# The row maximum of the attention scores in two reductions instead of one, with the score tile kept fixed

## The chip, the cores and the metric

The kernel runs on one core of one Trainium2 chip. The metric is the device time of one execution in microseconds; less is better. Before the change the median of three runs is 1004.71 us (1004.12 to 1005.11). The core has five engines that run side by side and wait for one another through semaphores: TensorE (PE, with weight loads shown as PEld), VectorE (DVE), ScalarE (ACT), GpSimd (POOL) and SyncE (SP), which issues most of the transfers (DMA).

## The reference

One block of a network over 2048 tokens of width 640: a layer norm with a modulation from a conditioning vector, attention in a sliding window of 256 tokens with 32 heads of 20 columns, a projection, a second layer norm, and a two-layer MLP with 1536 hidden columns. The part that matters here:

```
qkv = (x @ wqkv).reshape(B, S, 3, H, Dh)          # H = 32 heads, Dh = 20
scores = einsum("bhqd,bhkd->bhqk", q, k) * (Dh ** -0.5)
mask = (idx[:, None] - idx[None, :] >= 0) & (idx[:, None] - idx[None, :] < W)   # W = 256
p = softmax(where(mask, scores, -1e9))
o = einsum("bhqk,bhkd->bhqd", p, v)
...
x = x + ga * (o @ wo)
x = x + gb * MLP(layernorm(x) * (1 + cb) + sb)
```

The softmax needs the maximum of every row of the masked scores.

## The kernel before, in words

The work falls into a prologue (the first columns of q and k), an attention phase, and the MLP. In the attention phase the tokens come in two halves of 1024, the heads in eight quads of four, and the queries in blocks of 128. One step `t` of the main loop takes one block of queries of one quad. There are 128 such steps, and three things overlap in a step:

- `s_batch` (tile `s`): the scores of 128 queries against up to 384 keys, for four heads, by TensorE into PSUM. `s_max` then masks them on VectorE (`copy_predicated`, the mask of the block that leaves the window) and reduces them to the row maximum `nm` with one `tensor_reduce` over 256 columns of each of four heads (the 128 columns of the first key block are folded in by the masking copy).
- `e_batch` (tile `e`): 11 steps later (`LAG`), the same scores transposed, keys on the partitions, with the negated maximum brought in through two further rows of q. `e_mask` masks on VectorE, `e_exp` takes the exponential on ScalarE into `pt`, and GpSimd masks two further blocks.
- `pv_stage` (tile `o`): the product of `pt` with the values.

The rest of TensorE's time in a step goes to the projections of later columns (`pp`, `ppo`), which a plan spreads over the steps by tables of numbers (`EXTRA`, `EARLY`, `AFTER` and others). Neither the plan nor the tables are touched. Everything is recorded in program order on each engine, so an instruction that waits holds up all that stands behind it on its engine.

From step 11 to step 127 (117 steps) `width()` gives 384, and the tiles `s` and `e` have 4 x 384 = 1536 columns of 4 bytes each, which is three PSUM banks of 512 columns. Head slots 0 to 3 start at columns 0, 384, 768 and 1152. So slot 1 lies in banks 0 and 1, slot 2 in banks 1 and 2, and slot 3 wholly in bank 2. `cuts` splits a product where it crosses a bank. There is one tile `s` and one tile `e`: the products of the next step write the same columns that the reduction of this step reads.

The slots 0 and 1 use rows 0 to 59 (61 for `e`) of TensorE's array, the slots 2 and 3 rows 64 and up, so two products at a time can run side by side. `score_batch` orders them by the list `BOTH`. In a step with both tiles that gives, on TensorE's queue: three products of `e`, two of `s` (first 256 columns in bank 1, then 384 columns in bank 2), three of `e`, four of `s`. Where a step has no `e`, the list `ONE` gives six of `s`, and the first two are the same. Tiles are asked from a pool for every step, and the first product into a new tile waits for what used the old one (`reuse_waits="tile"`).

Of the kernel before, what the change touches and what calls it, by code (L numbers as in the profile page):

```python
# [9 lines left out]
F32 = mybir.dt.float32  # L10
# [3 lines left out]
ALU = mybir.AluOpType  # L14
AX = mybir.AxisListType
PSUM = bass.MemoryType.PSUM

P = 128
# [47 lines left out]

SUMS_LAST = [14, 18, 25, 31, 32, 42, 43, 46, 50, 52, 55, 58, 60, 61, 62, 63, 76, 77, 78, 79, 88, 90, 91, 94, 95, 99, 101, 102, 103, 105, 108, 109, 110, 111, 115, 116, 117, 120, 122, 126, 127, 131, 132, 133, 136, 139]
LEAST = 4
MOST = 10
MODS = [[9.5, 17.0], [16.75, 27.5], [70.5, 79.0]]  # L70
WOS = [88.75, 91.75, 99.25, 110.25, 112.0, 113.25, 116.0]
# [53 lines left out]
def block_kernel(ctx: ExitStack, tc: tile.TileContext, x, wqkv, wo, w1, b1, w2, b2, c, crow, wmod, wcol, sel, outT):  # L125
    core = tc.nc
    nc = Ordered(tc)
# [75 lines left out]
    pools = {}  # L203
# [327 lines left out]

    def score_banks(kind, name):
        n = width()
        t = pools[kind].tile([P, 4 * n], F32, tag=kind, name=name)
        return t, t.rearrange("p (h n) -> p h n", n=n)[:, :, 0:384]

    def width():
        return 384 if LAG <= now[0] < 2 * NQB * QUADS else 512  # L540
# [10 lines left out]
    def score_batch(batches):  # L551

        cut = []
        for n, (t, parts) in enumerate(batches):
            cut.append([
                [(n, at // 512, t[:, at:to], lhs, rhs(off, to - at)) for col, size, lhs, rhs in part for at, to, off in cuts(slot, col, size)]  # L560
                for slot, part in enumerate(parts)
            ])
        both = [{m[1] for m in c[0] + c[1]} & {m[1] for m in c[2] + c[3]} for c in cut]
        own = lambda n, slot: [m for m in cut[n][slot] if m[1] not in both[n]]
        shared = lambda n, slot: [m for m in cut[n][slot] if m[1] in both[n]]

        kinds = {
            (n, k): go
            for n in range(len(batches))
            for k, go in zip("abcdef", (shared(n, 0) + shared(n, 1), own(n, 1), own(n, 0), own(n, 3), own(n, 2), shared(n, 2) + shared(n, 3)))  # L570
        }
        order = BOTH if len(batches) == 2 else ONE
        queue = [(int(k in "def"), mm) for n, k in order for mm in kinds.get((int(n), k), ())]
        given = {}
        for i, (half, mm) in enumerate(queue):
            n, bank, out, lhs, rhs = mm
            if half and (n, bank) in given:
                assert not [1 for h, m in queue[i:] if not h and m[:2] == (n, bank)]
                tc.add_manual_dep(
                    nc.tensor.nop().ins, given.pop((n, bank)).name, in_order, reason="rows of the array share a bank"  # L580
                )
            ins = matmul(out, lhs, rhs, start=True, stop=True).ins
            if not half and bank in both[n]:
                given[n, bank] = ins

# [18 lines left out]
    def s_max(it, s, c0):  # L604

        data = negc.to_broadcast([P, 4, P]) if c0 else s[:, :, 0:P]
        nc.vector.copy_predicated(s[:, :, 2 * P : 384], masks["s"].to_broadcast([P, 4, P]), data)
        nc.vector.tensor_reduce(it["quad"]["nm"][:, :, it["key"][2]], s[:, :, max(c0, P) : 384], AX.X, ALU.max)

    def m_rows(it):  # L610
        half, quad, _, _ = it["key"]
# [561 lines left out]
    lo, hi = 4.0, 16.0  # L1173
    for _ in range(30):
        room = (lo + hi) / 2
        lo, hi = (lo, room) if lay_units(room)[0] <= LAST else (room, hi)
# [35 lines left out]
    for half in range(2):  # L1212
# [4 lines left out]
        for quad in range(QUADS):  # L1217
            if half or quad:
                js = range(4 * quad * DH // P, (4 * quad * DH + 4 * DH - 1) // P + 1)
                due = 8 * (half * QUADS + quad)  # L1220
                for c2 in range(2):
                    t = due + 4 * c2 - READ
                    for kind in range(2):
                        t = max([t, due - 8 * NSLOT + LAG + 8] + [over_at.get((kind, j, c2), -9) + 2 for j in js])
# [3 lines left out]
    for n, ((g, at), lo) in enumerate(zip(((2, 0), (4, 1), (3, 2)), MODS)):  # L1228
        steps, rows = mod_steps(g, at)
        spread(plan, [step(1, f) for f in steps], lo[0], lo[1])  # L1230
        t = int(lo[1])
        for f in rows:
            t = take_aside(t, f) + 1
    for ch, when in turns.items():
# [7 lines left out]
        t = when  # L1242
# [244 lines left out]
```

## Time and profile before

| | |
|---|---|
| median of 3 runs | 1004.71 us |
| the profiled execution's own time | 1004.25 us |
| its span, first to last instruction | 1002.5 us |
| busy: PE, PEld | 951.8 us (95%), 755.3 us (75%) |
| busy: DVE, ACT, POOL | 592.8 us (59%), 444.6 us (44%), 481.7 us (48%) |
| stretch 97 to 557 us (the 117 steps with three-bank tiles): PE, DVE busy | 433.80 us, 347.26 us of 460.00 |

How to read it: a line of the groups has the operation, its tiles as out<-in, shapes and count, then busy time, the mean of one in ns, and the idle time of the engine just before, with what ended it. A line of the timeline has start, length, engine and operation, and in brackets the idle time before it. Instructions next to each other with the same tiles are merged, with their count. All operations are recorded by one helper, so they all show as line L119 and are told apart by tiles. The busy time of PE contains ends that are modelled: a product that follows another closely overlaps it in the rows, so a short wait need not show as idle time.

### The profile page before, as it was taken

The numbers are of one execution on the slowest core, as the hardware profiler recorded it, in microseconds if no ns is written. First come the engines' busy times: TensorE is split into PE (matmuls) and PEld (weight loads), VectorE is DVE, ScalarE is ACT, GpSimd is POOL, SyncE is SP. The second block draws the span as 40 slices with busy tenths as digits, with TensorE's granted clock in tenths as the row PEclk, the third lists the DMA queues.
The fourth block names the chain that finished last, engine by engine and source line by source line (L and its number), as shares of the span: only waits on it lengthen the run. The fifth ranks groups of instructions, "written<-read, shape, count | busy, mean of one in ns | idle before, by whom it ended". The sixth has DMA issues, their size and how long they took to land.

```text
span 1002.5 us, 19950 instructions
## 1 busy us (share of the span) xinstructions
PE 951.8 (95%) x7737; PEld 755.3 (75%) x7737; DVE 592.8 (59%) x939; ACT 444.6 (44%) x781; POOL 481.7 (48%) x680
## 2 busy tenths in 40 slices
PE   8899999999999999999698879999999999999997
PEld 7777777777777677777476658888888888888886
DVE  6564867879677787767678644765444444433112
ACT  3724545566654544554345663343433343333122
POOL 4423655676864354644537844454543445442221
PEclk9999999999999999999899989999999999999999
DMA  8265878557678269834662144444422334124113
GB/s 301 91 215 144 280 239 263 169 163 212 198 231 260 86 178 277 234 101 159 190 184 67 52 127 136 154 131 139 132 86 84 94 129 127 40 64 147 53 45 113
DMA packets 99262, 152.81 MB, mean 152 GB/s; under 512 B 8897, under 2 KB 42145, under 8 KB 99169
## 3 DMA queue, kind: packets, MB, share of 16 engines
q1 hardware_dynamic: 89952, 143.16, 46.3%
q10 hardware_dynamic: 9216, 8.39, 2.6%
q8 instruction: 61, 1.00, 0.4%
q14 instruction: 33, 0.26, 0.1%
HBM read 99.17 MB, written 51.58 MB: 150 GB/s over the span
## 4 chain that ended last, share of the span: by engine, by line
PE 80%; DVE 9%; ACT 4%; issue 2%; DMA 2%; POOL 1%; SPq 0%; DVEq 0%; ACTq 0%; POOLq 0%
PE pp L119 16%; PE out L119 16%; PE h L119 16%; PE o L119 7%; PE e L119 7%; PE wo L119 6%; PE s L119 6%; DVE e L119 3%; ACT pt L119 3%; DVE nm L119 2%; PE ppo L119 2%; DVE s L119 1%; PE yt L119 1%; PE pv L119 1%; PE xt L119 1%
## 5 line engine op out<-in xcount | busy, mean ns | idle before, releaser
L119 POOL TENSOR_SCALAR_AFFINE_SELECT pt<-pt 128x512 f32<-128x512 f32 x192 | 129.2, 673 | 149.3 <-ACT pt L119 142.6
L119 ACT ACTIVATE pt<-e 128x1024 f32<-128x1024 f32 (+1 forms) x120 | 133.6, 1114 | 66.6 <-DVE e L119 63.3
L119 POOL TENSOR_TENSOR w2lo<-w2r,w2hi 128x640 fp32r<-128x640 f32 x48 | 75.8, 1580 | 166.9 <-ACT w2hi L119 166.7
L119 DVE TENSOR_REDUCE nm<-s 128x4 f32<-128x1024 f32 (+1 forms) x128 | 152.7, 1193 | 4.4
L119 PEld LDWEIGHTS e<-qbuf,kbuf 62*128 62x128 f32 x773 | 81.5, 188 | 57.5 <-ACT pt L119 33.1
L119 PE MATMUL e<-qbuf,kbuf 62*128 62x128 f32 (+2 forms) x773 | 108.0, 320 | 17.3 <-ACT pt L119 17.0
L119 PE MATMUL s<-kbuf,qbuf 60*128 60x128 f32 (+2 forms) x728 | 108.3, 312 | 10.3 <-DVE nm L119 7.4
L119 PE MATMUL pp<-hhi,whi 128*128 128x512 f32 x265 | 114.0, 430 | 0.9 <-ACT whi L119 0.7
L119 DVE COPY_PREDICATED e<-mask_t,e 128x512 f32<-128x512 uint32 x96 | 66.6, 694 | 77.5 <-PE e L119 66.8
L119 DVE CAST ghi<-g 128x512 fp32r<-128x512 f32 x48 | 27.1, 565 | 143.9 <-ACT g L119 143.8
L119 PE MATMUL pp<-hlo,whi 128*128 128x512 f32 x265 | 107.6, 406 | 3.1 <-POOL hlo L119 3.1
L119 PE MATMUL pp<-hhi,wlo 128*128 128x512 f32 x265 | 108.2, 408 | 0.0
L119 PE MATMUL o<-pt,vbuf 128*32 128x128 f32 x2688 | 102.1, 282 | 0.5 <-ACT oT L119 0.4
L119 PEld LDWEIGHTS s<-kbuf,qbuf 60*128 60x128 f32 x728 | 82.9, 187 | 21.7 <-DVE nm L119 5.4
L119 POOL TENSOR_TENSOR wlo<-wraw,whi 128x128 fp32r<-128x128 f32 x180 | 77.9, 463 | 39.9 <-ACT whi L119 32.0
L119 PE MATMUL out<-ghi,w2hi 128*128 128x512 f32 x240 | 96.2, 401 | 0.0
L119 PE MATMUL h<-yhi,w1hi 128*128 128x512 f32 x240 | 95.8, 399 | 0.0
L119 PE MATMUL out<-ghi,w2lo 128*128 128x512 f32 x240 | 94.1, 392 | 0.0
L119 PE MATMUL out<-glo,w2hi 128*128 128x512 f32 x240 | 94.0, 392 | 0.0
L119 PE MATMUL h<-ylo,w1hi 128*128 128x512 f32 x240 | 93.9, 391 | 0.0
L119 PE MATMUL h<-yhi,w1lo 128*128 128x512 f32 x240 | 93.9, 391 | 0.0
L119 ACT COPY oT<-o 128x128 f32<-128x128 f32 x128 | 33.8, 264 | 128.2 <-PE o L119 121.8
(169 smaller groups left out, 1840.8 us busy)
## 6 DMA issues: line engine op xcount, KB each, us to landing
w2r<-in_w SPq DMA_DIRECT2D x48, 320.0 KB
qbuf<-q_scr SPq DMA_DIRECT2D x60, 240.0 KB
wraw<-in_wqkv SPq DMA_DIRECT2D x37, 320.0 KB
kbuf<-k_scr SPq DMA_DIRECT2D x44, 240.0 KB
q_scr<-stage SPq DMA_DIRECT2D x20, 512.0 KB
k_scr<-stage SPq DMA_DIRECT2D x20, 512.0 KB
o_scr<-oT ACTq DMA_DIRECT2D x64, 128.0 KB
wm<-in_wmod SPq DMA_DIRECT2D x20, 320.0 KB
```

The costliest lines, as they stand in the source:

```text
L119: return self.tc.keep_in_program_order(op(*args, **kw))
```

## The change

Three things change, all for the steps in which `s` has three banks.

1. `s_max` reduces in two instructions: slots 0 to 2 (`CUT = 3`) and then slot 3. The columns read and the values written are the same.
2. The tile `s` is asked from its pool once and kept (`fixed`), so a step's products follow what they overlap in the tile and no longer a change of tile.
3. In `score_batch`, a product of `s` is declared free of a reduction that reads no bank which it writes. The first reduction reads columns 0 to 1151, banks 0 to 2. The second reads columns 1152 to 1535, bank 2. So the products into banks 0 and 1 stand behind the first reduction alone.

```diff
+CUT = 3
...
+    fixed, maxima = {}, []
+
     def score_banks(kind, name):
         n = width()
-        t = pools[kind].tile([P, 4 * n], F32, tag=kind, name=name)
+        if kind == "s" and n == 384:
+            if "s" not in fixed:
+                fixed["s"] = pools[kind].tile([P, 4 * n], F32, tag=kind, name=name)
+            t = fixed["s"]
+        else:
+            t = pools[kind].tile([P, 4 * n], F32, tag=kind, name=name)
         return t, t.rearrange("p (h n) -> p h n", n=n)[:, :, 0:384]
...
             ins = matmul(out, lhs, rhs, start=True, stop=True).ins
+            if n == len(batches) - 1 and width() == 384:
+                for red, banks in maxima:
+                    if bank not in banks:
+                        tc.declare_no_dep(ins, red, reason="no bank of the maximum")
...
-        nc.vector.tensor_reduce(it["quad"]["nm"][:, :, it["key"][2]], s[:, :, max(c0, P) : 384], AX.X, ALU.max)
+        del maxima[:]
+        n = width()
+        for lo, hi in ((0, CUT), (CUT, 4)) if n == 384 else ((0, 4),):
+            red = nc.vector.tensor_reduce(
+                it["quad"]["nm"][:, lo:hi, it["key"][2]], s[:, lo:hi, max(c0, P) : 384], AX.X, ALU.max
+            )
+            if n == 384:
+                maxima.append((red.ins, range(lo * n // 512, (hi * n - 1) // 512 + 1)))
```

What stands on VectorE's queue around one step of the second half (the reduction of step 109, the masks of step 110, `e1_4_3` and the scores behind it), before. The name in front of the arrow is what is written, and the bracket names the engines or transfers whose semaphores the instruction waits for:

```order
L119 COPY_PREDICATED e1_4_3_6328<-mask_t_73,e1_4_3_6328 128x4x128 [waits PE_49,Activation_49]
L119 COPY_PREDICATED s1_5_6_6329<-mask_t_73,s1_5_6_6329 128x4x128 [waits DVE_49,PE_49]
L119 TENSOR_REDUCE nm1_5_6034<-s1_5_6_6329 128x4 [waits DVE_49]
L119 COPY_PREDICATED e1_4_4_6400<-mask_t_73,e1_4_4_6400 128x4x128 [waits PE_49,Activation_49]
L119 COPY_PREDICATED s1_5_7_6401<-mask_t_73,s1_5_7_6401 128x4x128 [waits DVE_49,PE_49]
```

The same place after (the kept tile has the name of the step in which it was asked for, `s0_1_3`):

```order
L120 TENSOR_REDUCE nm1_5_6035<-s0_1_3_996 128x1
L120 COPY_PREDICATED e1_4_3_6329<-mask_t_73,e1_4_3_6329 128x4x128 [waits PE_49,Activation_49]
L120 COPY_PREDICATED s0_1_3_996<-mask_t_73,s0_1_3_996 128x4x128 [waits DVE_49,PE_49]
L120 TENSOR_REDUCE nm1_5_6035<-s0_1_3_996 128x3 [waits DVE_49]
L120 TENSOR_REDUCE nm1_5_6035<-s0_1_3_996 128x1
L120 COPY_PREDICATED e1_4_4_6401<-mask_t_73,e1_4_4_6401 128x4x128 [waits PE_49,Activation_49]
```

The second reduction waits for nothing of its own and stands directly behind the first; over the program VectorE has 117 instructions more.

TensorE's queue in the same step, before (`e1_4_3` is the transposed tile of this step, `s1_5_6` its scores, `qbuf` and `kbuf` hold q and k; `o1_4_0` is the product with the values that comes next):

```order
L119 MATMUL e1_4_3_6328<-qbuf0_96,kbuf0_99 128x128
L119 MATMUL s1_5_6_6329<-kbuf1_100,qbuf1_97 128x256 [waits DVE_49,PE_49]
L119 MATMUL s1_5_6_6329<-kbuf1_100,qbuf1_97 128x384
L119 MATMUL e1_4_3_6328<-qbuf0_96,kbuf0_99 128x128
L119 MATMUL e1_4_3_6328<-qbuf0_96,kbuf0_99 128x384
L119 MATMUL e1_4_3_6328<-qbuf0_96,kbuf0_99 128x256 [waits PE_49]
```

And after:

```order
L120 MATMUL e1_4_3_6329<-qbuf0_96,kbuf0_99 128x128
L120 MATMUL s0_1_3_996<-kbuf1_100,qbuf1_97 128x256 [waits DVE_49]
L120 MATMUL s0_1_3_996<-kbuf1_100,qbuf1_97 128x384 [waits DVE_49]
L120 MATMUL e1_4_3_6329<-qbuf0_96,kbuf0_99 128x128
L120 MATMUL e1_4_3_6329<-qbuf0_96,kbuf0_99 128x384
L120 MATMUL e1_4_3_6329<-qbuf0_96,kbuf0_99 128x256 [waits PE_49]
```

No product changes its place. The first score product loses its second wait (on TensorE's own semaphore) and keeps one on VectorE. The second score product, into bank 2, has a wait on VectorE of its own.

## The prediction

> **What bounds the kernel now.** I read the page first, then the stretch of the attention steps, then who waits for the reductions, then the timeline of single steps.
>
> ```profile
> span 1002.5 us, 19950 instructions
> PE pp L119 16%; PE out L119 16%; PE h L119 16%; PE o L119 7%; PE e L119 7%; PE wo L119 6%; PE s L119 6%; DVE e L119 3%; ACT pt L119 3%; DVE nm L119 2%; PE ppo L119 2%; DVE s L119 1%; PE yt L119 1%; PE pv L119 1%; PE xt L119 1%
> ```
>
> ```profile
> 97.00:557.00 460.00, 433.80 (x4861) 325.07 (x4862) 347.26 (x448) 243.35 (x453) 258.99 (x412) 0.99 0.64 193
> ```
>
> The second line is the chain of work that ended last. It is TensorE nearly throughout. Reductions (`DVE nm`) hold 2% of it, some 20 us or 16 of them at 1.23 us each. The third line is the stretch 97 to 557 us, in which the change acts (span, then busy PE, PEld, DVE, ACT, POOL): TensorE is idle for 26 us, VectorE for 113 us. So VectorE's load is not the bound. What counts is when a reduction lets TensorE go on.
>
> ```profile
>   PE s L119: 7.4, 14
>   PEld s L119: 5.4, 7
> ```
>
> These are the waits for `nm`: 12.8 us in 21 places. That understates it, since the ends of TensorE's products are modelled and cover short waits. I therefore paired each reduction's end with the first score product behind it. A step that is not held looks like this (VectorE's reduction, then on TensorE the first product of `e`, the first of `s`, the last of `e`):
>
> ```profile
> 299.69 1.23 DVE L119 TENSOR_REDUCE nm<-s 128x4 f32<-128x1024 f32 x1
> ...
> 301.02 0.45 PE L119 MATMUL e<-qbuf,kbuf 62*128 62x256 f32 x3
> 301.30 0.34 PE L119 MATMUL s<-kbuf,qbuf 60*128 60x256 f32 x2
> ...
> 301.56 0.35 PE L119 MATMUL e<-qbuf,kbuf 62*128 62x256 f32 x1
> ```
>
> The reduction is over at 300.92. TensorE comes by itself: 0.28 us from `e` to `s`, 0.26 from `s` to the last `e`. A held step:
>
> ```profile
> 480.33 1.23 DVE L119 TENSOR_REDUCE nm<-s 128x4 f32<-128x1024 f32 x1
> 482.48 0.70 DVE L119 COPY_PREDICATED e<-mask_t,e 128x512 f32<-128x512 uint32 x1 [0.93 <-PE e L119]
> ...
> 480.87 0.44 PE L119 MATMUL e<-qbuf,kbuf 62*128 62x256 f32 x3 [0.94 <-ACT pt L119]
> 481.70 0.44 PE L119 MATMUL s<-kbuf,qbuf 60*128 60x256 f32 x2 [0.39 <-DVE nm L119]
> ...
> 482.04 0.33 PE L119 MATMUL e<-qbuf,kbuf 62*128 62x256 f32 x1
> ```
>
> Here `s` follows `e` after 0.83 us and the reduction's end (481.56) after 0.14. The last `e` comes 0.34 after the first `s`, and only then can the mask of `e` start. This is a ring: mask of `e`, mask of `s`, reduction, two score products, rest of `e`, mask of `e`. In 51 of the 116 steps the first score product starts at one of three fixed distances behind the reduction's end, which is the sign of being held:
>
> - 0.14 to 0.15 us, 24 steps, from the first to the last of these:
>
> ```profile
> 104.84 1.23 DVE L119 TENSOR_REDUCE nm<-s 128x4 f32<-128x1024 f32 x1
> 106.21 0.45 PE L119 MATMUL s<-kbuf,qbuf 60*128 60x256 f32 x2
> ...
> 517.96 1.23 DVE L119 TENSOR_REDUCE nm<-s 128x4 f32<-128x1024 f32 x1
> 519.33 0.45 PE L119 MATMUL s<-kbuf,qbuf 60*128 60x256 f32 x2
> ```
>
> - 0.05 to 0.06 us, 17 steps, first and last, with the last `e` of the latter:
>
> ```profile
> 124.14 1.23 DVE L119 TENSOR_REDUCE nm<-s 128x4 f32<-128x1024 f32 x1
> 125.42 0.45 PE L119 MATMUL s<-kbuf,qbuf 60*128 60x256 f32 x2 [0.24 <-DVE nm L119]
> ...
> 529.17 1.23 DVE L119 TENSOR_REDUCE nm<-s 128x4 f32<-128x1024 f32 x1
> 530.45 0.45 PE L119 MATMUL s<-kbuf,qbuf 60*128 60x256 f32 x2
> ...
> 530.80 0.33 PE L119 MATMUL e<-qbuf,kbuf 62*128 62x256 f32 x1
> ```
>
> - 0.10 us, 10 steps, one in eight, where new q and k have landed. One in full (reduction, first and second score product, last `e`), and the last one:
>
> ```profile
> 360.29 1.23 DVE L119 TENSOR_REDUCE nm<-s 128x4 f32<-128x1024 f32 x1
> 361.62 0.54 PE L119 MATMUL s<-kbuf,qbuf 60*128 60x256 f32 x2
> ...
> 361.75 0.41 PE L119 MATMUL s<-kbuf,qbuf 60*128 60x384 f32 x1
> ...
> 362.06 0.33 PE L119 MATMUL e<-qbuf,kbuf 62*128 62x256 f32 x1
> ...
> 542.54 1.23 DVE L119 TENSOR_REDUCE nm<-s 128x4 f32<-128x1024 f32 x1
> 543.87 0.45 PE L119 MATMUL s<-kbuf,qbuf 60*128 60x256 f32 x2
> ```
>
> The three kinds go with the waits that the first score product has: VectorE and TensorE in all 24 of the first kind, VectorE last in all 17 of the second, transfers, VectorE and TensorE in the 10 of the third. A second wait costs 0.09 us when it is looked at after the first has come.
>
> **The change part by part.**
>
> *The two reductions.* Their length comes from the two shapes that the trace has:
>
> ```profile
> L119 DVE TENSOR_REDUCE nm<-s 128x4 f32<-128x1024 f32 x111 | 136.1, 1226 | 3.8
> ...
> L119 DVE TENSOR_REDUCE nm<-s 128x4 f32<-128x512 f32 x6 | 4.2, 693 | 0.2
> ```
>
> 512 elements cost 533 ns, so 1.04 ns each, and 160 ns are fixed. Three heads (768) take 960 ns, one head (256) 427 ns, together 1387, which is 160 more than now. The second waits for nothing, and such a neighbour starts before the first is over:
>
> ```profile
> 231.09 1.23 DVE L119 TENSOR_REDUCE nm<-s 128x4 f32<-128x1024 f32 x1
> 232.23 0.88 DVE L119 BATCH_NORM_STATS2 st<-xt 128x6 f32<-128x320 f32 x2
> ```
>
> 232.23 against an end of 232.32: 0.09 us overlap. So the first ends 0.27 us sooner than the one does now, the second 0.07 later. The ends for this unknown: 0 later (no fixed part at all) and 0.16 later (no overlap). I take 0.07 since the overlap row is a reduction with a neighbour behind it.
>
> *The first score product* may start 0.27 us sooner in a held step. It is worth little by itself: the second score product stands right behind it and now waits for the second reduction, and three products of `e` stand behind that one on TensorE. Nothing is let past. The gain is what remains between the second score product and the last `e` once the first is out of the way. The 0.10 kind shows it: there the second started 0.13 behind the first, and the last `e` came 0.31 after it, against 0.34 where both start together. So 0.03.
>
> *The waits.* With the kept tile the first score product has lost its wait on TensorE, and the second has VectorE as its last wait, so I take the 0.05 of the second kind for both. Time from the old reduction's end to the last `e` after the change: 0.07 + 0.05 + 0.31 = 0.43 us. Before:
>
> - first kind 0.14 + 0.34 = 0.48: 24 x -0.05 = -1.2 us
> - second kind 0.05 + 0.35 = 0.40: 17 x +0.03 = +0.5 us
> - third kind 362.06 - 361.52 = 0.54: 10 x -0.11 = -1.1 us
>
> *VectorE's other work.* 117 x 0.07 = 8 us more, in 113 us of idle time. It costs where VectorE runs on behind the reduction and the chain stays on it, as here in the chain's own rows:
>
> ```profile
> 231.09 1.23 DVE nm L119
> 232.32 0.80 DVE st L119 x2
> ```
>
> The chain leaves a reduction this way or through a delayed mask in perhaps four steps: +0.3 us (0 to 1.1, all 16 chain reductions). Steps not held pay nothing: their product comes 0.2 to 2 us after the reduction, more than 0.07.
>
> *Transfers, ScalarE, GpSimd, the MLP* keep their instructions; what comes earlier or later in attention moves the rest as a block.
>
> Sum: -1.2 + 0.5 - 1.1 + 0.3 = -1.5 us. The profiled execution has 1004.25 us, 1.75 more than its span, and lies 0.46 under the median of the runs; on the median it gives 1003.2 us. About 0.2%, 2 us, is what a measurement here can tell from no change.
>
> [...] The overlap of 0.09 us above decides the sign. [...]
>
> **The rivals.**
>
> *Slower: the second reduction pays its whole fixed part.* Then it ends 0.16 later: first kind +0.04 x 24 = 1.0, second +0.12 x 17 = 2.0, third -0.02 x 10 = -0.2, VectorE's other work 4 x 0.16 = 0.6, and the ring grows: +3.4, 1008.1 us. It decides from a second reduction ending 0.10 us late (51 x 0.03 more than I take eats the 1.5). For it: both reductions read PSUM and write neighbouring words of `nm`, a pair that the trace does not show. Against: the overlap row.
>
> *No change: what is gained in the ring is waited for elsewhere.* `e` itself waits for the exponential before it:
>
> ```profile
> PEld e L119 <- ACT pt L119: 23.0, 39, 1.4
> ```
>
> Half of the -1.8 lost there gives 1004.1 us. Against: the exponential starts from the mask of `e`, which moves with the ring. That the first product still waits for the second reduction would also end here; the separate wait of the product behind it speaks against that.
>
> *Clearly faster: the whole first product leaves the block.* In a held step the last `e` needs 0.34 us where a step that is not held needs 0.26. If the early product also spares this restart, each of the 51 gains 0.05 to 0.08 more, some 3 us: 1000.2 us.
>
> **How the numbers follow.** My forecast, 1001.5 to 1004.5, has 0.45; its centre lies 0.5 us inside the bound for "same", so I split it 0.22 faster, 0.23 same. Slower rival 0.27, no change 0.16 (0.13 same, 0.03 slower), clearly faster 0.12. That gives faster 0.34, same 0.36, slower 0.30. The range leaves out half of the clearly faster case below 1000.5 and a part of the slower one above 1007.8.
>
> **What would show it.** Right: a first reduction near 960 ns and a second near 430 that starts some 0.09 us before the first ends; in held steps a pause between the first and the second score product, the second 0.05 us behind the second reduction; distances of 0.14 gone; waits of TensorE for `nm` about as long as now, on the second product. Wrong: the second reduction starting after the first's end or lasting well over 430 ns; steps of the 0.05 kind lengthened by more than 0.1; a mask of `e` that starts later behind reductions followed by other VectorE work.

## The result, and the profile after

In runs taken in turn on one chip, the kernel before took 1004.02 us in the median (1000.90 to 1005.11, 12 runs) and the changed one 1000.98 us (1000.53 to 1002.67, 12 runs). The ratio of the means is 0.9979, with a 95% interval of 0.9969 to 0.9988: faster by 0.2%, some 2 us. The forecast was 1003.2 us, 1.5 under the median of its three runs. The sign was right, and the time lies in the whole range (1000.5 to 1007.8), though 0.5 us below the 1001.5 to 1004.5 of the forecast itself. Most of the reason was not right, as the rest shows: that the time came out near was mostly luck.

The profiled execution after took 1000.98 us, with a span of 999.0. The page's span, its busy times, and its chain of work:

```profile
span 999.0 us, 20009 instructions
PE 955.0 (96%) x7737; PEld 757.2 (76%) x7737; DVE 601.7 (60%) x1056; ACT 444.8 (45%) x781; POOL 480.9 (48%) x680
PE pp L120 16%; PE out L120 16%; PE h L120 16%; PE o L120 7%; PE e L120 6%; PE wo L120 6%; PE s L120 6%; DVE e L120 4%; ACT pt L120 3%; PE ppo L120 2%; DVE nm L120 1%; PE yt L120 1%; PE xt L120 1%; PE pv L120 1%; DMA wc<-in_wcol 1%
```

VectorE has 1056 instructions instead of 939 and is 9 us busier. Reductions hold 1% of the chain instead of 2%. The groups by line have the two reductions:

```profile
L120 DVE TENSOR_REDUCE nm<-s 128x3 f32<-128x768 f32 x111 | 106.4, 959 | 3.8
L120 DVE TENSOR_REDUCE nm<-s 128x1 f32<-128x256 f32 x111 | 46.0, 415 | 0.0
```

The held step that the prediction shows in full (reduction at 480.33 us there) looks like this in the timeline after. VectorE's rows come first, then TensorE's:

```profile
480.70 0.96 DVE L120 TENSOR_REDUCE nm<-s 128x3 f32<-128x768 f32 x1
481.57 0.41 DVE L120 TENSOR_REDUCE nm<-s 128x1 f32<-128x256 f32 x1
482.82 0.70 DVE L120 COPY_PREDICATED e<-mask_t,e 128x512 f32<-128x512 uint32 x1 [0.83 <-PE s L120]
...
481.71 0.38 PE L120 MATMUL s<-kbuf,qbuf 60*128 60x256 f32 x1
...
482.04 0.44 PE L120 MATMUL s<-kbuf,qbuf 60*128 60x384 f32 x1
...
482.38 0.33 PE L120 MATMUL e<-qbuf,kbuf 62*128 62x256 f32 x1
```

The second reduction starts 0.09 us before the end of the first (481.66) and is over 1.28 to 1.29 us after the start of the first, where the single one takes 1.23. The overlap is 0.08 to 0.09 us in all 117 steps of this trace, and in the 111 with 256 columns a head it is 1.29 us in the mean from the first start to the last end. The first score product comes 0.05 us behind the first reduction. The second score product comes 0.06 behind the second reduction (481.98). The last `e` follows the second score product after 0.34. So from the start of the reduction to the last `e` it takes 482.38 - 480.70 = 1.68 us, against 482.04 - 480.33 = 1.71 before. This held step, of the first kind, has gained 0.03 us, where 0.05 were forecast.

Where the 3.5 us between the two spans lie is read from four reductions (steps 12, 104, 107 and 113) and from VectorE's last work. The reductions after:

```profile
105.39 0.96 DVE L120 TENSOR_REDUCE nm<-s 128x3 f32<-128x768 f32 x1
...
460.24 0.96 DVE L120 TENSOR_REDUCE nm<-s 128x3 f32<-128x768 f32 x1
...
473.54 0.96 DVE L120 TENSOR_REDUCE nm<-s 128x3 f32<-128x768 f32 x1
...
499.44 0.96 DVE L120 TENSOR_REDUCE nm<-s 128x3 f32<-128x768 f32 x1
```

Before, step 12 is at 104.84 (shown in the prediction), and the other three are:

```profile
459.90 1.23 DVE L119 TENSOR_REDUCE nm<-s 128x4 f32<-128x1024 f32 x1
...
473.14 1.23 DVE L119 TENSOR_REDUCE nm<-s 128x4 f32<-128x1024 f32 x1
...
501.22 1.23 DVE L119 TENSOR_REDUCE nm<-s 128x4 f32<-128x1024 f32 x1
```

VectorE's last instructions before, with the moves of TensorE's last results (`out`), and the transfers from 990 to 1004 us: the busy share of the DMA engines in tenths, in 40 slices of 0.35 us, and the instruction transfer among them between 997 and 998 us (packets, MB, share of 16 engines):

```profile
994.50 2.11 DVE L119 SCALAR_TENSOR_TENSOR xr<-out,gb,xr 128x512 f32<-128x512 f32 x3 [2.21 <-PE out L119]
996.89 1.41 DVE L119 SCALAR_TENSOR_TENSOR xr<-out,gb,xr 128x512 f32<-128x512 f32 x2 [0.28 <-issue]
...
DMA  0000000000000000059999946936940000000000
...
q14 instruction: 1, 0.01, 6.5%
```

The same after:

```profile
992.08 3.47 DVE L120 SCALAR_TENSOR_TENSOR xr<-out,gb,xr 128x512 f32<-128x512 f32 x5 [2.21 <-PE out L120]
...
DMA  0000000000499999999950000000000000000000
```

| stretch, us | before | after | difference |
|---|---|---|---|
| start of the span to step 12 | 104.84 | 105.39 | +0.55 |
| step 12 to 104: attention with held steps | 355.06 | 354.85 | -0.21 |
| step 104 to 107 | 13.24 | 13.30 | +0.06 |
| step 107 to 113 | 28.08 | 25.90 | -2.18 |
| step 113 to the first of the last five moves | 493.28 | 492.64 | -0.64 |
| from there to the end of the span | 8.0 | 6.9 | -1.1 |

The 92 steps from 12 to 104, most of those in which the change was to gain, have 0.2 us of the 3.5. The start of step 12 lies anywhere from 104.2 to 105.4 us in the fourteen profiles of this case. The biggest piece is one place between steps 107 and 113, where new weights are prepared (`whi_late`, `wlo_late`) and TensorE waits for them. The windows of the granted clock there, before (start and end, length, busy PE, PEld, DVE, ACT, POOL, granted clock, DMA share, GB/s):

```profile
487.40:490.80 3.40, 0.73 (x2) 0.30 (x2) 1.12 (x1) 1.96 (x3) 1.16 (x1) 1.00 0.70 213
490.80:494.20 3.40, 2.96 (x14) 2.22 (x15) 2.21 (x2) 1.72 (x4) 3.33 (x4) 0.50 0.23 73
494.20:497.60 3.40, 3.40 (x33) 2.35 (x31) 2.78 (x4) 1.28 (x3) 2.51 (x3) 0.50 0.32 95
```

And after:

```profile
487.50:490.90 3.40, 0.84 (x3) 0.41 (x4) 1.36 (x3) 2.51 (x5) 1.77 (x3) 1.00 0.62 174
490.90:494.30 3.40, 3.40 (x22) 2.42 (x26) 2.75 (x3) 1.17 (x2) 3.33 (x3) 0.50 0.57 150
494.30:497.70 3.40, 3.40 (x41) 2.50 (x34) 2.29 (x4) 1.63 (x4) 3.09 (x5) 1.00 0.21 61
```

Both wait through a window with TensorE busy for 0.7 to 0.8 of 3.4 us, and get half the clock in the next. Before, that next window is busy for 2.96 us and a second half-clock window follows. After, it is busy for all 3.40 and the full clock follows. Whether this belongs to the change is a question for the experiments.

### The profile page after: what moved, and what is told of

Its sections match the earlier page's. It is cut to its first block, busy times and chain, and to the rows that moved or that the text cites. A ratio compares the mean times of both kernels' runs of the same rounds, so it can differ in the third digit from the quotient of the medians.

```text
span 999.0 us, 20009 instructions
## 1 busy us (share of the span) xinstructions
PE 955.0 (96%) x7737; PEld 757.2 (76%) x7737; DVE 601.7 (60%) x1056; ACT 444.8 (45%) x781; POOL 480.9 (48%) x680
## 4 chain that ended last, share of the span: by engine, by line
PE 80%; DVE 9%; ACT 5%; issue 2%; DMA 2%; POOL 1%; SPq 0%; ACTq 0%; DVEq 0%; POOLq 0%
PE pp L120 16%; PE out L120 16%; PE h L120 16%; PE o L120 7%; PE e L120 6%; PE wo L120 6%; PE s L120 6%; DVE e L120 4%; ACT pt L120 3%; PE ppo L120 2%; DVE nm L120 1%; PE yt L120 1%; PE xt L120 1%; PE pv L120 1%; DMA wc<-in_wcol 1%
## 5 line engine op out<-in xcount | busy, mean ns | idle before, releaser
L120 DVE TENSOR_REDUCE nm<-s 128x1 f32<-128x256 f32 (+2 forms) x245 | 160.1, 694 | 4.4
L120 PE MATMUL e<-qbuf,kbuf 62*128 62x128 f32 (+2 forms) x773 | 113.6, 323 | 16.6 <-ACT pt L120 16.4
L120 PEld LDWEIGHTS e<-qbuf,kbuf 62*128 62x128 f32 x773 | 84.2, 188 | 57.0 <-ACT pt L120 32.9
L120 PE MATMUL s<-kbuf,qbuf 60*128 60x128 f32 (+2 forms) x728 | 114.8, 312 | 6.0 <-DVE nm L120 3.2
L120 PEld LDWEIGHTS s<-kbuf,qbuf 60*128 60x128 f32 x728 | 88.6, 187 | 17.8 <-DVE nm L120 7.7
```

The costliest lines, as they stand in the source:

```text
L120: return self.tc.keep_in_program_order(op(*args, **kw))
```

## The experiments

All were timed against the kernel before on the same chip. Three stretches of each profile tell more than the times, since single runs of one kernel spread over up to 8 us:

| kernel | step 12 to 104 | step 107 to 113 | last moves to end | median us (runs), of before | ratio, 95% interval |
|---|---|---|---|---|---|
| before, first profile | 355.06 | 28.08 | 8.0 | | |
| changed, first profile | 354.85 | 25.90 | 6.9 | 1000.98 (12), 1004.02 | 0.9969 to 0.9988 |
| kept tile alone | 352.90 | 24.66 | 8.0 | 999.08 (11), 1003.53 | 0.9942 to 0.9973 |
| two reductions alone | 359.47 | 27.43 | 6.9 | 1004.86 (12), 1003.53 | 1.0011 to 1.0040 |
| kept tile and two reductions, no release | 357.74 | 25.99 | 6.9 | 1003.35 (12), 1003.21 | 0.9989 to 1.0011 |
| before, 24 products more | 354.97 | 30.01 | 7.9 | 1004.84 (12), 1003.53 | 1.0012 to 1.0042 |
| changed, 24 products more | 354.92 | 27.02 | 6.9 | 1001.82 (12), 1003.53 | 0.9983 to 1.0016 |
| before, 117 settings, new tile | 355.21 | 27.69 | 6.9 | 1005.59 (12), 1003.21 | 1.0002 to 1.0031 |
| before, 117 settings, old tile | 355.08 | 24.77 | 6.9 | 1001.85 (11), 1003.32 | 0.9972 to 1.0001 |
| kept tile, 117 settings, new tile | 352.68 | 27.73 | 6.9 | 1003.11 (12), 1003.21 | 0.9984 to 1.0011 |
| kept tile, 117 settings, old tile | 352.88 | 26.42 | 6.9 | 999.13 (5), 1003.32 | 0.9930 to 0.9968 |
| changed again | 355.17 | 24.94 | 6.9 | 1000.83 (12), 1003.21 | 0.9963 to 0.9985 |
| before, against itself | 355.00 | 26.45 | 8.0 | 1001.58 (12), 1003.39 | 0.9975 to 1.0008 |
| kept tile, all of `e` first | 363.45 | 28.50 | 8.0 | 1013.18 (4), 1003.32 | 1.0079 to 1.0112 |

The first column repeats to 0.2 or 0.3 us: five profiles with the attention code of before have 354.97 to 355.21, three of the changed one 354.85 to 355.17, three with the kept tile alone 352.68 to 352.90. That makes it the measure for what the change does in attention. The second column does not repeat at all.

**The parts one by one.** The kept tile alone, with one reduction:

```diff
+        if kind == "s" and n == 384:
+            if "s" not in fixed:
+                fixed["s"] = pools[kind].tile([P, 4 * n], F32, tag=kind, name=name)
+            t = fixed["s"]
```

> Kept score tile alone: one reduction over all four heads as before, no product declared free of anything. Two theories. Ring theory (the gain of the change lies in the steps in which a reduction holds TensorE, as the prediction has it): the first score product loses its second wait, 0.147 us behind the reduction's end becomes 0.055 in 24 steps, 0.102 becomes 0.055 in 10; the stretch from the reduction of step 12 to that of step 110 (378.97 us before, 378.76 after) falls by about 2.5 us, to 376.5, and the time by as much, to about 1001.5 us. Clock theory (the change gained 0.2 us in the held steps; the rest is one window of halved TensorE clock less at the late projection near 490 us): the stretch may fall as well, but the time follows the number of halved windows of 3.4 us behind 490 us, 1.7 us each, 1000 to 1004 us.

Measured: the stretch from step 12 to 104 is 2.2 us shorter, and at 999.08 us the kernel is faster than the one before and, by the median, than the changed one. That is below what either theory had named. Against the kernel before it gains some 4.2 us in the mean; 2.2 of them lie in the stretch, and the rest was not traced. Its interval touches that of the change. A held step of its timeline (reduction, first score products, last group of `e`):

```profile
457.38 1.23 DVE L119 TENSOR_REDUCE nm<-s 128x4 f32<-128x1024 f32 x1
...
458.66 0.44 PE L119 MATMUL s<-kbuf,qbuf 60*128 60x256 f32 x2
458.88 0.45 PE L119 MATMUL e<-qbuf,kbuf 62*128 62x384 f32 x3
```

The first score product comes 0.05 us behind the reduction's end (458.61), as the prediction took for a product that has only VectorE to wait for. The 0.14 kind is rare there: 30 of 41 held steps are at 0.05 to 0.06 us.

The two reductions alone, with a tile from the pool for every step and all products behind both:

```diff
-        nc.vector.tensor_reduce(it["quad"]["nm"][:, :, it["key"][2]], s[:, :, max(c0, P) : 384], AX.X, ALU.max)
+        for lo, hi in ((0, 3), (3, 4)) if width() == 384 else ((0, 4),):
+            nc.vector.tensor_reduce(
+                it["quad"]["nm"][:, lo:hi, it["key"][2]], s[:, lo:hi, max(c0, P) : 384], AX.X, ALU.max
+            )
```

> Two reductions alone: the tile is asked for in every step as before, so the first score product waits for both reductions and keeps its second wait. Both theories: the second reduction ends 0.06 us later than the one did, in each held step, so the stretch from step 12 to step 110 grows by 51 x 0.06 = 3 us to 382. Ring theory: time about 1007 us. Clock theory: 1007 us if the windows behind 490 us are as before, up to 2 us less or more by them.

Measured: the stretch is 4.4 us longer. Of this 1.0 falls between step 34 and 35, in a window with half the clock at 190 us.

The change without its third part, so that the first score product waits for both reductions:

```diff
-            if n == len(batches) - 1 and width() == 384:
-                for red, banks in maxima:
-                    if bank not in banks:
-                        tc.declare_no_dep(ins, red, reason="no bank of the maximum")
```

> The change with its third part taken back: kept tile and two reductions, but both score products wait for the second reduction. The measure is the stretch from the reduction of step 12 to that of step 110: 378.97 us before, 378.75 with the whole change, 377.02 with the kept tile alone. Theory of the prediction (the ring adds up by its distances): the first product starts 0.07 + 0.05 us behind the old reduction's end and the last e 0.34 later, 0.46 in all, which is nearly what the whole change does, so the stretch is 378.5 to 379.0, the release of the first product is worth nothing, and the time is 1000.5 to 1002. Rival (costs of the parts add up): two reductions alone made the stretch about 4 us longer and the kept tile alone 2 us shorter, so the stretch is 380.5 to 381.5, the release is worth 2 us, and the time is 1002.5 to 1004. In both the tail behind the last out product is 4.7 us and not 5.8, if that goes by the number of VectorE's instructions.

Measured: 357.74 us, 2.7 more than before; to step 110 it is 381.65. Costs that add up (the rival) describe it better than the ring's distances, and the release is worth 2.5 to 2.9 us in these profiles. But some 0.9 of that is a half-clock window at 189 us, in the row before last here:

```profile
182.40:185.80 3.40, 3.40 (x45) 2.48 (x43) 2.09 (x3) 0.98 (x3) 1.30 (x3) 1.00 0.94 341
185.80:189.20 3.40, 2.09 (x33) 1.49 (x33) 3.30 (x10) 2.77 (x6) 1.75 (x5) 0.99 0.07 17
189.20:192.60 3.40, 3.40 (x12) 2.38 (x12) 3.07 (x8) 0.68 (x2) 1.77 (x3) 0.50 0.66 165
192.60:196.00 3.40, 3.40 (x41) 2.48 (x40) 2.82 (x5) 1.87 (x3) 2.75 (x6) 1.00 0.94 343
```

TensorE waits for a reduction at 186 us in the kernel before too (0.69 us busy of the 2 from 186 to 188). Half the clock follows there in the two kernels whose two reductions hold all products, and in no other. Why is not shown: their windows were busy for 2.01 and 2.09 us, but one that was busy for 2.07 us, from 184.0 us in the second profile of the kernel before, was followed by the full clock.

To see the ring itself, all steps from 12 to 104 were taken whose product starts within 0.2 us behind the reduction that it waits for, and the mean was formed of the distance from the end of the last reduction to the last `e`. To it belongs the 0.065 us by which two reductions end later than one:

| kernel | held steps | last `e` behind the last reduction | with the later end | change x steps | measured, less half-clock windows |
|---|---|---|---|---|---|
| before | 41 | 0.467 | 0.467 | | |
| kept tile | 41 | 0.414 | 0.414 | -2.2 | -2.2 |
| two reductions | 43 | 0.463 | 0.528 | +2.6 | +3.4 |
| both, no release | 43 | 0.417 | 0.482 | +0.6 | +1.8 |
| the whole change | 40 | 0.401 | 0.466 | 0.0 | -0.2 |

The steps counted here are not all held in the strict sense. In the whole change the second score product starts 0.05 to 0.06 us behind the second reduction in 28 of the 40; in the other 12 TensorE comes to it by itself, 0.07 to 0.17 us behind.

So the ring's arithmetic is right for the kept tile and for the whole change, and short by 0.8 to 1.2 us for the two that let nothing go. Half a microsecond of that is one place. Behind the reduction at step 47 VectorE scales `xt`, twice. The operation by its tile (shortest, median and longest in ns, first and last start), before and after:

```profile
L119 DVE TENSOR_SCALAR xt<-xt,mv,rs x2: 606/770/935, 240.4 to 240.9; 128x640 f32<-128x640 f32 x2
```

```profile
L120 DVE TENSOR_SCALAR xt<-xt,mv,rs x2: 916/992/1067, 241.2 to 242.2; 128x640 f32<-128x640 f32 x2
```

At that step these two take 1.06 to 1.08 and 0.92 us in all kernels with two reductions, and 0.60 and 0.93 in all with one. The mask of `e` stands behind them, and the lag against before grows by 0.5 us at the next step (0.20 to 0.71 after, 1.98 to 2.50 with nothing released). The whole change has this half microsecond too, and makes it up later: its lag falls from 0.71 us at step 48 to -0.22 at step 104. The long form is not a matter of the two reductions alone: at the pair before, behind step 35, two profiles with one reduction have it too (the kernel before with 24 products more, and the kept tile with 117 settings in a new tile, both below). There too it costs 0.5 us at the next step, and that is made up by step 46.

In the ring the release is worth 0.016 us in a held step (0.417 to 0.401). What else it saves is not told apart by these runs.

**The clock.** To see whether the gain between steps 107 and 113 goes with TensorE's idle window, 24 products of the identity matrix (48 instructions in the trace), whose result nothing reads, were put into step 111 of the kernel before and of the changed one:

```diff
-WARM = {(130, 1): 2}
+WARM = {(130, 1): 2, (111, 2): 24}
```

> The kernel before with 24 products of the identity matrix added on TensorE in step 111, ahead of the late projection, where TensorE is idle for 3 to 5 us (486.9 to 491.2 us); their result is read by nothing. Ring theory: no change within 1 us. Clock theory: the window from 487.4 to 490.8 us no longer falls low enough, the two halved windows from 490.8 to 497.6 us go, 2 to 3.4 us less: 1000.5 to 1002 us.

> The changed kernel with the same 24 products in step 111. Ring theory: as far below the kernel before with the 24 products as the change is below the kernel before, about 2 to 3 us. Clock theory: the one halved window from 490.9 to 494.3 us goes, 1.7 us less, and what remains between this kernel and the one before with the 24 products is 1 us or less.

Measured: 1004.84 and 1001.82 us, 3.0 apart as without the products (2.3 in the means). Neither theory's time for the first of the two came, and the pair does not decide between them, since the products had a cost of their own. They did not fit into TensorE's wait:

```profile
487.98 7.23 PE L119 MATMUL warm<-idn 128*128 128x128 f32 x48
495.36 0.47 PE L119 MATMUL pp_late<-hhi,whi_late 128*128 128x512 f32 x1
```

The late projection starts 22.3 us behind step 107 here, and 16.5 in the kernel before (19.4 and 15.6 in the changed kernel with and without the products). Nor did they settle the clock: it was still at half from 484.6 to 491.4 us in the profile of the one, and at no place near in that of the other.

The changed kernel was then profiled again, and the kernel before was run against itself:

> The changed kernel once more, profiled anew beside the kernel before on the same chip as the other three. If the 2.3 us that its first profile gained between step 110 and the end of attention belong to the change, they are there again (step 110 to 127 takes 70.5 to 71.5 us against 73.2). If they came from where the stretches of half clock fell in the two profiles, this one may show 70 to 75 us there. The stretch from step 12 to step 110 is 378.7 to 378.9 us and the tail 4.7 us in either case; the time is 1000.5 to 1002.5.

> The kernel before, unchanged, against itself, to see how far a difference of medians goes without any change. If what three profiles of the same attention program showed between step 107 and step 113 (0, -0.4 and -3.3 us against the first profile) is chance, this one falls anywhere between -3.5 and +2 there; the stretch from step 12 to step 104 is 355.0 to 355.2 us and the tail 5.7 to 5.8 us in any case. The medians of the two should agree within 1 us. If this profile and the runs agree with the kernel before by 0.3 us, the 0.5 to 1 us that the changed kernel has beyond its tail is its own; if they differ by 0.7 us or more, it is not.

Measured: the changed kernel has 354.85 and 355.17 us from step 12 to 104, and 25.90 and 24.94 from 107 to 113. From step 110 to 127 its second profile has 69.5 us, below what either reading had named, and 379.57 from step 12 to 110, with half clock from 478.7 us on. The kernel before has 28.08 in its first profile. The two rows of its second, for steps 107 and 113:

```profile
473.20 1.23 DVE L119 TENSOR_REDUCE nm<-s 128x4 f32<-128x1024 f32 x1
...
499.65 1.23 DVE L119 TENSOR_REDUCE nm<-s 128x4 f32<-128x1024 f32 x1
```

That is 26.45 us. A third profile of the same attention code, with instructions added only in the MLP (below), has 24.77:

```profile
472.83 1.23 DVE L119 TENSOR_REDUCE nm<-s 128x4 f32<-128x1024 f32 x1
...
497.60 1.23 DVE L119 TENSOR_REDUCE nm<-s 128x4 f32<-128x1024 f32 x1
```

So the same instructions take 24.8 to 28.1 us there. Two things differ. One is where the half clock lies: from 490.8 for 6.8 us, from 491.2 for 3.4, and from 478.0 for 13.7 us in these three. The other is when the late weights are ready: their conversion (`whi_late`) starts 15.70, 15.40 and 13.92 us behind step 107. TensorE's first product with them, in the three:

```profile
489.62 0.50 PE L119 MATMUL pp_late<-hhi,whi_late 128*128 128x512 f32 x1 [2.73 <-ACT whi_late L119]
...
489.38 0.50 PE L119 MATMUL pp_late<-hhi,whi_late 128*128 128x512 f32 x1 [2.44 <-ACT whi_late L119]
...
488.54 0.80 PE L119 MATMUL pp_late<-hhi,whi_late 128*128 128x512 f32 x1
```

The profile with the longest half clock has no wait for the weights, and the shortest time. What makes the weights come sooner in one is not shown. The 2.2 us that the changed kernel's profile gains at that place are not shown to be the change's. The same goes for the 0.64 us behind it: of the 47 intervals between the MLP's blocks of `h`, those from the second on agree within 0.1 us in each between the two profiles, and the first differs by 0.63, beside half-clock stretches between 583 and 597 us. In the two profiles of the kernel before it differs by 1.16 (5.99 and 4.83). Against itself the kernel before came out 1.8 us apart in the medians and 0.9 in the means.

**The end.** The 1.1 us behind the last products are different: 7.9 to 8.0 us in all five profiles with VectorE's count of before, 6.9 in all nine with 117 instructions more. Of the 1.1, 0.3 lie in VectorE's last five moves (3.80 and 3.47 us from the first start to the last end) and 0.8 behind them. (The expectations call it the tail and count from the start of the last product of `out`, 5.8 and 4.7 us.) So 117 settings of one column to zero, which nothing reads, were put on VectorE in the MLP's gaps, first in a new tile:

```diff
+    pad = const.tile([P, 1], F32, name="pad")
...
+            for _ in range(0 if ch == 0 else 4 if ch == 1 and f < 9 else 3):
+                nc.vector.memset(pad, 0.0)
```

> The kernel before, with 117 settings of one column to zero on VectorE (read by nothing) in the gaps of the MLP phase, where VectorE is idle for 5 us at a time. VectorE then has as many instructions as in the changed kernel, and nothing else is changed. Theory of the instructions' place (the 1.1 us that the changed kernel gains behind its last out product come from where its last instructions lie, not from what the change does in attention): the tail is 4.7 us as in the changed kernel, against 5.8, the 0.28 us pause before VectorE's last two instructions is gone, and the time is 0.8 to 1.3 us below that of the kernel before. Rival (the tail depends on how the transfers at the end meet): the tail stays at 5.7 to 5.8 us and the time within 0.5 us of the kernel before.

> The kept tile alone, with the same 117 settings of one column in the MLP phase. Theory of the instructions' place: the tail is 4.7 us against 5.8 with the kept tile alone, and the time 997.5 to 999, the fastest so far and 2 to 3 us below the changed kernel. Rival (the tail is not a matter of the count): 998.5 to 1000, tail 5.8. In both the stretch from step 12 to step 110 is 377.0 us.

Measured: the end falls to 6.9 us in both, with no pause before the last two moves. But the times are 1005.59 and 1003.11, since the MLP's steps became longer, 3.6 us in all; the last eleven take 6.93 us instead of 6.80. Two successive ones, by VectorE's row:

```profile
945.69 0.43 DVE L119 CAST ghi<-g 128x512 fp32r<-128x512 f32 x1 [5.50 <-ACT g L119]
...
952.62 0.43 DVE L119 CAST ghi<-g 128x512 fp32r<-128x512 f32 x1 [5.50 <-ACT g L119]
```

The theory of the place was right and the edit had a cost of its own. Its next form writes a column of a tile that the kernel has and no longer needs:

```diff
+            for _ in range(0 if ch == 0 else 4 if ch == 1 and f < 9 else 3):
+                nc.vector.memset(c_sb[:, 0:1], 0.0)
```

> As the one before with the 117 settings, but they write a column of a tile that the kernel has anyway and no longer needs, so that no other tile lies elsewhere in memory. Theory (with the new one-column tile the tiles behind it moved by its size, and the 20 products from the first of h on in each step of the MLP took 0.233 us instead of 0.227 for that): a step of the MLP takes 6.80 us again and not 6.93, the tail is 4.7 us, and the time is the kernel's before less 1.1 us: 0.8 to 1.5 us below it. Rival (the settings themselves slow TensorE): 6.93 us again, and 1.5 to 2.5 us above the kernel before. If the changed kernel's gain of 2.0 to 2.6 us in the means is its tail and the luck of the half-clock stretches alone, this kernel is within 0.5 us of it, 1001 to 1002.

> The kept tile alone with the same 117 settings into a column that is no longer needed. Theories as for the kernel before with these settings: place in memory: 6.80 us in a step of the MLP, stretch from step 12 to step 104 352.7 to 352.9 us (355.1 before), tail 4.7, so 3.4 us below the kernel before, 999 to 1000, by the sum of these, or down to 997.5 if the kept tile's first time (4.2 us below, with 2.2 of it in that stretch) repeats. Rival: 6.93 us in a step of the MLP and 1002 to 1003.

Measured: 6.80 us a step again, in the kernel before with these settings:

```profile
939.76 0.43 DVE L119 CAST ghi<-g 128x512 fp32r<-128x512 f32 x1 [5.37 <-ACT g L119]
...
946.56 0.43 DVE L119 CAST ghi<-g 128x512 fp32r<-128x512 f32 x1 [5.37 <-ACT g L119]
```

With 117 idle instructions and no other change the kernel before takes 1001.85 us in the median and 1001.69 in the mean, 1.3 under the mean of its own runs beside it (1003.01). That fits the 1.1 us of the end, though the interval just reaches 1. It is 0.9 to 1.0 us above the two medians of the changed kernel, which were timed apart from it. The kept tile with them takes 999.13 us, ratio 0.9949 (0.9930 to 0.9968), faster than both kernels; against the kept tile alone (0.9958) the intervals overlap.

**The order of the products.** If the ring is so costly because the last three products of `e` stand behind score products that wait for the reduction, they can be put ahead of all scores (one reduction, kept tile):

```diff
-BOTH = "0a 0d 0b 1a 1d 0e 0c 0f 1c 1e 1f 1b".split()
+BOTH = "0a 0d 0b 0e 0c 0f 1a 1d 1c 1e 1f 1b".split()
```

> The kept tile, one reduction, and the order of the list BOTH changed so that all six products of e stand ahead of the scores on TensorE. Theory of the ring (a held step is long because the last three products of e stand behind score products that wait for the reduction, and the mask of e waits for them): the last e no longer waits for the reduction, the mask of e starts right behind the reduction on VectorE, 0.4 us earlier in each of the 40 to 50 held steps, and the stretch from step 12 to step 104 falls by 3 us or more below 352.9 us, until TensorE itself or the exponential sets the pace; time 993 to 997. Rival (the scores come later instead and with them mask, reduction and the row maxima, so that the reduction ends later against the next products): the stretch is 352 to 357 us and the time 998 to 1005.

Measured: 1013.18 us, and the stretch is 10.6 us longer than with the kept tile alone. Neither the theory nor its rival had so much. One step of its timeline (mask of `e` on VectorE, then the copy of `o` and the exponential on ScalarE):

```profile
466.34 0.70 DVE L119 COPY_PREDICATED e<-mask_t,e 128x512 f32<-128x512 uint32 x1 [1.82 <-PE e L119]
...
467.70 0.27 ACT L119 COPY oT<-o 128x128 f32<-128x128 f32 x1 [1.16 <-PE o L119]
467.86 1.03 ACT L119 ACTIVATE pt<-e 128x1024 f32<-128x1024 f32 x1
```

The same step before:

```profile
458.57 0.69 DVE L119 COPY_PREDICATED e<-mask_t,e 128x512 f32<-128x512 uint32 x1 [1.56 <-PE e L119]
...
459.56 0.27 ACT L119 COPY oT<-o 128x128 f32<-128x128 f32 x1 [0.78 <-PE o L119]
459.72 1.03 ACT L119 ACTIVATE pt<-e 128x1024 f32<-128x1024 f32 x1
```

The exponential stands behind the copy of `o` on ScalarE, and the products of `o` stand behind the scores on TensorE. With all of `e` first the mask comes early and the scores late, so the exponential starts 1.52 us behind its mask instead of 1.15. This is one step in full. From step 12 to 104 an exponential starts 1.13 us behind the mask of `e` before it in the mean, against 1.02 with the kept tile alone. Over 92 steps that is of the size of the 10.6 us; no run separated it from other causes.

## Why the prediction was right, and where it was wrong

- **The two reductions.** 960 and 427 ns forecast, 959 and 415 measured; 0.09 us of overlap forecast and measured; an end 0.07 us later forecast, 0.06 measured. The overlap row of another pair of operations (232.23 against 232.32) was enough for this one (481.57 against 481.66).
- **The first score product.** In the step shown it goes 0.27 us ahead and lets nothing past, as forecast. In most steps it does not even use its head start: of the 40 counted from step 12 to 104 it starts 0.05 to 0.06 us behind the first reduction in 6, and in the others TensorE reaches it by itself, 0.1 to 0.5 us behind.
- **The waits.** 0.05 to 0.06 us behind the reduction that holds it, as forecast, for the second product in the 28 steps in which it is held. The distance of 0.14 is gone, and its price of 0.09 us fits the kept tile alone, 2.2 us shorter by 41 x 0.053.
- **The step that failed** is "So 0.03": from the second score product to the last `e` it was to take 0.31 us, by the 0.10 kind, where the second product starts 0.13 behind the first. It takes 0.34, as when both start together, in 24 of the 28 steps just named, with the first product anywhere from 0.05 to 0.33 us ahead of the second. So a head start of the first product does not shorten this stretch. What made it 0.31 in that kind is not shown; there both products were released by the transfers and the second stood 0.13 behind without a wait of its own. Taking 0.03 off each gain gives 24 x -0.02, 17 x +0.06 and 10 x -0.08: -0.3 us in place of -1.8, before VectorE's other work. With the +0.3 of that work the sum is 0.0. Measured from step 12 to 104: -0.2, -0.1 and +0.1 in three profiles.
- **VectorE's other work.** +0.3 forecast, with 1.1 as its end. What was found are scalings of `xt` that became longer, not later alone: 0.5 us at step 35 and again at step 47, both made up later.
- **"What comes earlier or later moves the rest as a block"** was wrong twice. The last five moves of the kernel took 1.1 us less because 117 instructions more stood ahead of them on VectorE. And between steps 107 and 113 one kernel differs from itself by 3.3 us.
- **The base.** One profile and three runs of the kernel before were taken as its time. Its profile has 28.08 us between steps 107 and 113, where three others with the same attention code have 27.69, 26.45 and 24.77, so it stood at the long end. The comparison with itself shows that 12 runs against 17 can differ by 0.9 us in the mean without cause.
- **The rivals.** The slower one (the second reduction at its whole fixed part) is refuted by the overlap. In attention the outcome is that of the "no change" rival, but for another reason than it named: the gain was not lost to a wait of `e` for the exponential, it was not there. The clearly faster rival named a time (1000.2) near the measured one for a reason that is not there: the last `e` needs 0.34 us still.

In sum: of the 2.1 to 2.4 us in the means, 1.1 are at the end by the count of instructions, which is shown. Attention from step 12 to 104 gives 0.1, no more than its profiles spread. For the rest, some 0.8 to 1.2 us, no place was found that the kernel before does not also reach on its own; whether a part of it belongs to the change stays open.

## What to carry to other kernels

Ask of a gain whether its stretch repeats, by a second profile of the same program: here the stretch with the change repeated to 0.3 us and showed no gain, while the kernel's end and a place that differs from profile to profile made the time. Before an instruction is split so that a reader goes sooner, look at what stands directly behind that reader on its queue; if it still waits for the second part, the first part's head start is worth little (0.016 us a held step here). Of several parts of a change, run each alone: one of the three here (the kept tile) made the kernel 0.4% faster, and with the two reductions attention was back where it had been.

## What the runs showed of the hardware that was not expected

- **Within a trace the granted clock changed at whole multiples of 3.41 us from one change to the next.** Between 100 and 900 us it changes at 490.77, 497.59, 589.75 and 596.58 us before, and at 490.92, 494.33, 583.08 and 593.32 after. The half-clock stretches there last 3.41, 6.83 or 10.24 us, and the two traces' changes lie 0.15 us off each other's grid. Windows of that length with 0.73 us (487.40 to 490.80 before), 0.84 (487.50 to 490.90 after) and 2.09 us (185.80 to 189.20 with nothing released) of busy TensorE were followed by half the clock, one with 2.37 (183.60 to 187.00 before) by the full one. But no bound in busy time comes out of the traces: 2.09 us was followed by half the clock, and 2.01 (582.93 to 586.34 before) by the full one. Nor does one for the way back: a half-clock window that was busy for 3.03 us (593.17 to 596.58 before) was followed by the full clock, while with the 117 settings in the old tile the clock stayed at half from 478.0 to 491.7 us, though from 479.69 us on TensorE's products leave no gap of more than 0.15 us there.
- **The end of this kernel depends on how many instructions VectorE had before it.** With 939 (7.9 to 8.0 us to the end) VectorE pauses 0.28 us before its last two moves, and an instruction transfer runs among the last results' transfers (6.5% of the 16 engines from 997 to 998 us before, 6.8% from 990 to 991 with the kept tile alone). Before the change their rate, in slices of 0.35 us, is 357 to 375 GB/s at first and then swings between 105 and 392. With 1056 (6.9 us) there is no pause, and after the change the rate is 357 to 386 GB/s in every slice between the first and the last, and the instruction transfer comes behind the last result. These two counts alone were run. Whether the instruction transfer causes the pause and the lower rate was not tried.
- **A new tile of one column made TensorE slower.** With it, products from the first of `h` on took 0.233 us from start to start instead of 0.227, some 20 in each step of the MLP, 0.13 us in each of the last eleven steps; with the same instructions on an old tile they did not. That the tiles behind it lay at other addresses is the difference left, and it was not tried by itself.
- **The same scaling on VectorE came in two lengths:** 0.61 us before and 1.07 after for the first of the two at step 47, beside a selection on GpSimd that ran at that time in both (1.81 us for two before, 1.48 after). It began 0.07 us later behind its reduction there (1.14 and 1.21 us), but that is not shown as the cause: at step 35 both lengths stand at the same distance from the selection (0.11 us; 0.60 us before, 1.10 with the 24 products). What sets the length is not shown.
